# A fused retention, two-expert mixture and SoLU kernel: the second expert's weights, rows and list places, and the last weights, in another order

## The chip, the cores and the metric

The kernel runs on one core of one Trainium2 chip, in one launch. The metric is the device time of one execution in microseconds (us), the median over runs. The core has five instruction streams that run in parallel and meet at semaphores: PE (TensorE, matmuls), DVE (VectorE), ACT (ScalarE), POOL (GpSimd) and SP (SyncE). Each stream is worked off strictly in the order in which it was written. SP, ACT and POOL also issue DMAs. An instruction that waits holds up all that stand behind it on the same stream.

## The reference

Three layers follow one another on 1536 tokens of 512 numbers (2 sequences of 768, 8 heads of 64).

```python
# 1. retention: a state per head that decays by gamma and takes k v^T at each step
for t in range(S):
    state = gamma * state + einsum('bhd,bhe->bhde', k[:, :, t], v[:, :, t])
    y[:, :, t] = scale * einsum('bhd,bhde->bhe', q[:, :, t], state)
x = y.transpose(0, 2, 1, 3).reshape(B * S, H * D)
# 2. mixture of 8 experts, two for each token, chosen by noisy logits
noisy_logits = x @ w_gate + log1p(exp(x @ w_noise)) * noise
top2, top2_w = two largest, softmax of the two
for e in range(8):
    out[mask] += top2_w[mask, k, None] * (maximum(x[mask] @ w1[e], 0) @ w2[e])
# 3. SoLU block: 512 -> 1024 -> 512
h = x @ w_in
solu = h * softmax(h)
ln = (solu - mean) / sqrt(var + 1e-6) * g_ln
return ln @ w_out
```

`w_in` and `w_out` come as 64-bit floats and are converted on DVE while the experts run (`convert()`). Every weight and every operand of the two large layers is split into a high and a low part, and each product is three matmuls (high by high, high by low, low by high).

## The kernel before

**Units.** The weights are 72 units of 512 KB, eight for each expert (four of `w1`, four of `w2`) and eight for the last layer. `load_unit` starts the DMA of a raw unit (tile `wr`, four buffers), `split_unit` makes the high part `wh` on ACT (L202) and the low part `wl` on DVE (L203); ten split units fit. `feed(split_to, load_to)` advances both counters, and `advance(e, j)` calls it once for each quarter of an expert. A load can start only when the split of the unit four before it has released the buffer. Which expert runs when is known only from the counts: `turns()` orders the experts (`turn_ix`), and from expert 1 on the address of a load comes from a register that the issuing engine reads from `turn_ix` (L170). Units 8 to 11, the `w1` of expert 1, are issued by POOL; all others by SP.

**Attention**, 12 tiles of 128 tokens, one turn of the loop at L708 for each tile i: `from_state` (old state times queries), `kv` (state update, L435; copied by ACT as `S`), `from_chunk` (L449, with the masked scores `pm`; DVE scales its result to `xT`, L451, by a table `fade` that ACT makes in `table(c)`, L368), `scale_v(i + 2)` (the values times their decay, one half on POOL, the other on ACT), `scores(i + 1)` (L405, masked by DVE at L409), and `rows_logits(i)` (L461: turns the tile into rows and makes its logits; ACT copies both out, and SP stores the rows to `xd`). Between these stand the steps of the choice of experts, for four groups of tiles (0 to 3, 4 to 7, 8 and 9, 10 and 11): `route(g)`, called four times for each group (logits and noise; first half of a polynomial; its second half and the two largest, which gives `chosen`; their indices), `rank(g)` (PE counts places, L582), `slots(g)` (DVE works out the place of each token in its expert's list), `first_rows(g)` (DVE marks the tokens of expert 0, tiles `oh`, L527) and `scatter(i)` (POOL writes a tile's token numbers to the lists, two indirect DMAs).

**Expert 0** starts early: 192 of its rows come from tiles 0 to 7 (`list_rows(0)` finds them by matmuls with `oh`, POOL gathers them, `first_xt(0, .)` turns them on PE) and run through `w1` in one full-precision pass, `hidden(0, f, ...)` for f = 0 to 7 (L671 with `xe`). Its later 256 rows are listed and turned meanwhile (`list_rows(1)`, `first_xt(1, .)`, split on DVE at L572), and follow as eight more `hidden` steps with split operands. Each `hidden` step ends with `hh` on ACT (L675) and `hl` on DVE (L676); for expert 0 they use two buffers of bank `b`.

**Experts 1 to 7.** `second(e, j)`, j = 0 to 3, is an expert's second product (L1030, eight steps of 12 matmuls). During it the next expert's rows are made ready: `load_xg` on POOL (list entries, then rows; for expert 1 four gathers `xr`, L975), and `xg_t(e + 1, d)`, d = 0 to 3, which for expert 1 turns the rows on PE into bank `a` (two buffers), with ACT (`xh`, L995) and DVE (`xl`, L996) behind it. Only then does `hidden(e + 1, ...)` start.

**The end.** The last expert's results are made as rows (L1115, b = 0 to 2), stored to `yg` (L1101), gathered for each token by POOL (`gather`, L751), mixed (`mix`, ACT L761 and DVE L762), turned (`x2_t`, L771) and sent through the last layer, 12 tiles, in a software pipeline. The last two units of weights (four rows of `w_out` blocks) are split by `last_weights` into room that expert 7's operands leave.

Of the kernel before, what the change touches and what calls it, by code (L numbers as in the profile page):

```python
# [44 lines left out]
def retnet_moe_solu(ctx, tc, qT, kT, k, v, w_gate, w_noise, noise, w1, w2, w_in, w_out, g_ln,  # L45
# [110 lines left out]
    def load_unit(u):  # L156
# [7 lines left out]
        q = nc.gpsimd if e == 1 and j < 4 else nc.sync  # L164
        if e == E:
            wa, wb = w_in, w_out
        else:
            wa, wb = w1, w2
            if e and (e, q) not in turn_of:
                turn_of[e, q] = nc.values_load(turn_ix[:1, e:e + 1], engines=[q.engine], min_val=0, max_val=E - 1)  # L170
            n = bass.DynSlice(turn_of[e, q], 1) if e else slice(0, 1)
            wa, wb = (w[n].rearrange("o r c -> (o r) c") for w in (wa, wb))
# [105 lines left out]
    for half in range(2):  # L278
# [8 lines left out]
                   allow_small_or_imprecise_dtypes=True)  # L287
    number = const.tile([128, NT], F16, name="number")
# [107 lines left out]
    def scores(i, between=None):  # L396
# [9 lines left out]
        if between:  # L406
            between()
# [64 lines left out]
    def choose(g):  # L472
# [3 lines left out]
        t = rt.tile([128, 8, 4, E], F32, tag="rt", name="rt")  # L476
        th, r, ab, nl = (t[:, n, :m] for n in range(4))
        lg = rt.tile([128, 4, 2 * E], F32, tag="lg", name="lg")[:, :m]
# [15 lines left out]
        ix = rt.tile([128, 4, 8], U32, tag="ix", name="ix")  # L494
# [7 lines left out]
        pk = rt.tile([128, 4, 2, E], F32, tag="pk", name="pk")  # L502
# [9 lines left out]
    def first_rows(g):  # L512
# [10 lines left out]
        for s in range(m):  # L523
# [3 lines left out]
            V.tensor_scalar(t[:, lo:], col[:, lo:], s0[:, s:s + 1], None, op0=OP.is_equal)  # L527
# [173 lines left out]
    ROUTE = {3: (0, 0), 4: (0,), 5: (0,), 7: (1, 1), 8: (1,), 9: (2,), 10: (2,)}  # L701
    SCATTER = {5: (0,), 6: (1,), 7: (2,), 8: (3,)}
# [5 lines left out]
    for i in range(NT):  # L708
# [5 lines left out]
        from_chunk(i)  # L714
        if i == 11:
            route(2)
        scale_v(i + 2)
        scores(i + 1, (lambda: list_rows(0, range(EARLY_TILES), "a0")) if i == 10 else None)
        rows_logits(i)
        if i == 5:  # L720
            rank(0, "a1")
        if i == 9:
            rank(1, "a1")
            first_rows(1)
        if i == 11:
# [147 lines left out]
    def last_weights():  # L873
# [5 lines left out]
        for n in range(4):  # L879
# [30 lines left out]
    route(1)  # L910
    route(3)
    first_xt(0, 0)
    first_xt(0, 2)
    first_rows(2)
    slots(1)
    for n in range(4, 6):
        scatter(n)
    route(3)
    route(3)
    raw0 = [raw_t[d] for d in range(KD)]  # L920
    for f in range(KF):
        evacuate = hidden(0, f, slice(0, EARLY), ("c0", "c1", "b", "b")[f % 4])
        if f == 1:
            list_rows(1, range(NT - 2), "a1")
# [10 lines left out]
        if f == 4:  # L935
            route(2)
            slots(2)
            scatter(8)
            scatter(9)
        if f == 5:  # L940
            route(3)
            slots(3)
            scatter(10)
            scatter(11)
    feed(4, 8)
    for p in range(2):
        first_xt(1, 2 * p)
    turns()
# [72 lines left out]
    def second(e, j, py):  # L1021
# [20 lines left out]
    for e in range(E - 1):  # L1042
# [51 lines left out]
    feed(n_units - 2, n_units)  # L1094
# [9 lines left out]
    conv_ctx.close()  # L1104
    m2_ctx = ExitStack()
    fr = m2_ctx.enter_context(tc.tile_pool(name="fr", bufs=2, side="right", reuse_waits="tile"))
    for b in range(3):
# [26 lines left out]
    solu(0)  # L1134
    x2_t(2)
# [6 lines left out]
    z_turn(1)  # L1142
# [170 lines left out]
```

## Time and profile before

| | |
|---|---|
| median of 3 runs | 537.77 us (546.83, 537.77, 534.22) |
| the profiled execution | 533.07 us, its span 531.4 us |
| granted TensorE clock, mean over the span | 0.976 of full speed |
| PE busy | 505.0 us (95%) |
| DVE busy | 373.8 us (70%) |
| ACT busy | 217.6 us (41%) |
| POOL busy | 190.1 us (36%) |
| chain that ended last | PE 73%, DMA 3%, issue 2%, POOL 1%, DVE 1% |

The span is from the first to the last instruction; the execution's own time has 1.7 us more around it. "Busy" counts what an engine worked on; a matmul whose operands are late is not busy, one that runs at the lower clock is busy for twice as long. The clock is granted at one of two levels, 2.4 GHz (1.00) and 1.2 GHz (0.50); a value between them in a stretch means that both were granted in it. Stages by the timeline: attention to about 62 us, expert 0's early rows to 81, its later rows to 99, its second product and the turn of expert 1's rows to 130, experts 1 to 7 to 363, the rest the last expert's rows and the last layer.

### The profile page before, as it was taken

To read this page: it belongs to the slowest core of one execution; us is meant where nothing else is said; L and a number is where in the kernel's file an instruction comes from. 1 tells how busy PE (TensorE), PEld (TensorE's weight loads), DVE (VectorE), ACT (ScalarE), POOL (GpSimd) and SP (SyncE) were. 2 spreads that over 40 slices of the span, in tenths; PEclk is the share of its full clock that TensorE was granted. 3 is DMA by queue.
4 is the path that set the end of the run, shared out by engine and by line. 5 is a ranking of instruction groups with operands and counts; after the bars stand their busy time and mean duration, and the time that the engine had idled before them with its cause. 6 is when DMAs were issued, how large, how long until landed. Compare 5 with 4: busy or idle time off the path is not lost.

```text
span 531.4 us, 8949 instructions
## 1 busy us (share of the span) xinstructions
PE 505.0 (95%) x3216; PEld 459.3 (86%) x3216; DVE 373.8 (70%) x741; ACT 217.6 (41%) x426; POOL 190.1 (36%) x291
## 2 busy tenths in 40 slices
PE   8989897967999999999999999999799999999996
PEld 7877787957999999999999999998578888888885
DVE  4487867635888986987888879885348865666640
ACT  4565342432432442434434334435425543343441
POOL 3126258657475715507327000000423523311120
PEclk9999978997999999999999999999989999999999
DMA  8899407087576695766867857667522754553331
GB/s 249 303 303 345 156 22 257 21 270 255 199 179 218 229 269 187 221 177 222 237 224 227 245 178 203 197 164 222 174 85 81 223 172 141 162 175 100 99 120 45
DMA packets 60130, 100.36 MB, mean 189 GB/s; under 512 B 10896, under 2 KB 28400, under 8 KB 60080
## 3 DMA queue, kind: packets, MB, share of 16 engines
q1 hardware_dynamic: 52144, 83.84, 50.9%
q0 software_dynamic: 6592, 15.54, 9.9%
q8 instruction: 27, 0.44, 0.3%
q10 hardware_dynamic: 1344, 0.34, 0.3%
q14 instruction: 23, 0.19, 0.1%
HBM read 76.99 MB, written 22.70 MB: 188 GB/s over the span
## 4 chain that ended last, share of the span: by engine, by line
PE 73%; DMA 3%; issue 2%; POOL 1%; DVE 1%; ACT 0%; POOLq 0%; ACTq 0%; DVEq 0%
PE c L1030 22%; PE d L790 13%; PE b L897 12%; PE b L671 12%; PE a L671 12%; DMA wr<-in_moe_w_dram 1%; PE c L1115 1%; PE a L771 1%; DMA yg<-y 1%; DMA y<-yg,slot_y 1%; DVE wl L203 0%; POOL y L751 0%; PE a L843 0%; POOL wr L184 0%; PE a L989 0%
## 5 line engine op out<-in xcount | busy, mean ns | idle before, releaser
L975 POOL DMA_INDIRECT xq<-xd,rows x78 | 86.2, 1106 | 61.0 <-issue 60.3
L203 DVE TENSOR_TENSOR wl<-wr,wh 128x1024 fp32r<-128x1024 f32 x68 | 81.8, 1220 | 12.1 <-ACT wh L202 11.8
L1030 PE MATMUL c<-hh,wh 128*128 128x448 f32 (+5 forms) x224 | 79.8, 356 | 0.0
L1030 PE MATMUL c<-hl,wh 128*128 128x448 f32 (+5 forms) x224 | 79.5, 355 | 0.0
L1030 PE MATMUL c<-hh,wl 128*128 128x448 f32 (+5 forms) x224 | 79.4, 355 | 0.0
L202 ACT ACTIVATE wh<-wr 128x1024 fp32r<-128x1024 f32 x68 | 69.9, 1050 | 13.4 <-DMA wr<-in_moe_w_dram 12.1
L751 POOL DMA_INDIRECT y<-yg,slot_y x24 | 24.0, 1001 | 92.4 <-DMA yg<-y 86.7
L671 PE MATMUL b<-xh,wh 128*128 128x256 f32 (+7 forms) x144 | 48.0, 339 | 2.5 <-DVE hl L676 2.3
L671 PE MATMUL b<-xh,wl 128*128 128x256 f32 (+7 forms) x144 | 47.6, 337 | 0.0
L1030 PEld LDWEIGHTS c<-hh,wh 128*128 128x128 f32 x224 | 42.7, 191 | 1.2
L1030 PEld LDWEIGHTS c<-hh,wl 128*128 128x128 f32 x224 | 42.6, 190 | 1.2
L1030 PEld LDWEIGHTS c<-hl,wh 128*128 128x128 f32 x224 | 42.6, 190 | 1.2
L790 PE MATMUL d<-wh,x2h 128*128 128x512 f32 x96 | 40.1, 418 | 0.3 <-ACT x2h L774 0.3
L675 ACT ACTIVATE hh<-b 128x256 fp32r<-128x256 f32 (+8 forms) x40 | 18.7, 467 | 52.7 <-PE b L671 52.5
L790 PE MATMUL d<-wh,x2l 128*128 128x512 f32 x96 | 39.0, 406 | 0.2 <-DVE x2l L775 0.2
L671 PE MATMUL a<-xh,wh 128*128 128x448 f32 (+6 forms) x112 | 39.0, 348 | 0.0
L671 PE MATMUL a<-xh,wl 128*128 128x448 f32 (+6 forms) x112 | 38.9, 347 | 0.0
L790 PE MATMUL d<-wl,x2h 128*128 128x512 f32 x96 | 38.7, 404 | 0.0
L995 ACT ACTIVATE xh<-xt 128x428 fp32r<-128x428 f32 (+5 forms) x24 | 13.0, 540 | 56.1 <-DVE xt L993 56.1
L675 ACT ACTIVATE hh<-a 128x448 fp32r<-128x448 f32 (+6 forms) x28 | 14.3, 512 | 47.0 <-PE a L671 47.0
L817 POOL TENSOR_SCALAR st<-st 128x1 f32<-128x1 f32 x12 | 2.3, 190 | 85.4 <-ACT ee L814 85.4
L671 PE MATMUL b<-xl,wh 128*128 128x256 f32 (+7 forms) x144 | 31.2, 339 | 0.2 <-DVE xl L572 0.2
(226 smaller groups left out, 1114.9 us busy)
## 6 DMA issues: line engine op xcount, KB each, us to landing
wr<-in_moe_w_dram SPq DMA_DIRECT2D x60, 512.0 KB, 5.6
zd<-zs SPq DMA_DIRECT2D x40, 128.0 KB, 2.3
zc<-zd SPq DMA_DIRECT2D x10, 512.0 KB, 4.0
raw<-in_moe_w_in_dram SPq DMA_DIRECT2D x8, 512.0 KB, 5.0
raw<-in_moe_w_out_dram SPq DMA_DIRECT2D x8, 512.0 KB, 4.8
yg<-yr SPq DMA_DIRECT2D x16, 208.0 KB, 3.9
qt<-in_qT_dram SPq DMA_DIRECT2D x12, 256.0 KB, 4.7
vt<-in_v_dram SPq DMA_DIRECT2D x12, 256.0 KB, 5.4
```

Of the source, the lines that this page charges most:

```text
L202: nc.scalar.activation(hi, t, AF.Copy)
L203: nc.vector.tensor_sub(lo, t, hi)
L671: nc.tensor.matmul(p, w[:, 0, f * 128:(f + 1) * 128], x[:, d, c], start=(n == 0), stop=(n == len(terms) - 1))
L675: nc.scalar.activation(hh[:, f, c], p, AF.Relu)
L751: nc.gpsimd.indirect_dma_start(out=t, out_offset=None, in_=yg[:upto], in_offset=bass.IndirectOffsetOnAxis(ap=slot_y[:, i, s:s + 1], axis=0))
L771: nc.tensor.transpose(p[:, d * 128:(d + 1) * 128], t[:, d * 128:(d + 1) * 128], ident)
L790: nc.tensor.matmul(PH[i][:, s, :], x[:, c], w[:, 0, f], start=(n == 0), stop=(n == 3 * KD - 1))
L897: nc.tensor.matmul(p, z[:, f * 128:(f + 1) * 128], w_rows(f, n)[:, c], start=(m == 0), stop=(m == len(terms) - 1))
L975: nc.gpsimd.indirect_dma_start(out=x[:, b] if e > 1 else xr_t[e][b], out_offset=None, in_=src[:], in_offset=bass.IndirectOffsetOnAxis(ap=r ...
L995: nc.scalar.activation(hi, t, AF.Copy)
L1030: nc.tensor.matmul(py[d][:, :CAPS[e]], c, h[:, f, :CAPS[e]], start=(f == 0 and n == 0), stop=(f == KF - 1 and n == 2))
L1115: nc.tensor.matmul(py, h[:, f, c], w[:, f % 2], start=(f == 0 and n == 0), stop=(f == KF - 1 and n == 2))
```

## The change

The diff cut to its core. Line numbers after `@@` are those of the two files.

```diff
@@ load_unit
-        q = nc.gpsimd if e == 1 and j < 4 else nc.sync
+        q = nc.sync
...
@@ constants
+    col_h = const.tile([128, CAPS[0]], F16, name="col_h")
+    nc.vector.tensor_copy(col_h, col)
...
@@ first_rows
-            V.tensor_scalar(t[:, lo:], col[:, lo:], s0[:, s:s + 1], None, op0=OP.is_equal)
+            V.tensor_scalar(t[:, lo:], col_h[:, lo:], s0[:, s:s + 1], None, op0=OP.is_equal)
...
@@ the loop over attention's tiles
-    ROUTE = {3: (0, 0), 4: (0,), 5: (0,), 7: (1, 1), 8: (1,), 9: (2,), 10: (2,)}
-    SCATTER = {5: (0,), 6: (1,), 7: (2,), 8: (3,)}
+    SCATTER = {6: (0,), 7: (1,), 8: (2,), 9: (3,), 10: (4,), 11: (5,)}
...
         from_state(i)
         kv(i)
-        from_chunk(i)
-        if i == 11:
-            route(2)
-        scale_v(i + 2)
-        scores(i + 1, (lambda: list_rows(0, range(EARLY_TILES), "a0")) if i == 10 else None)
-        rows_logits(i)
-        if i == 5:
+        if i == 6:
             rank(0, "a1")
         if i == 9:
             rank(1, "a1")
+        if i == 11:
+            route(2)
+        from_chunk(i)
+        if i == 1:
+            table(1)
+        if i == 11:
+            rank(2, "a1")
+            first_xt(0, 0)
+            first_xt(0, 2)
+            first_rows(2)
+        scores(i + 1)
+        rows_logits(i)
+        if i and i % 2 == 0 and i + 2 < NT:
+            table(i // 2 + 1)
+        if i in (3, 4, 5, 6):
+            route(0)
+        if i == 6:
+            slots(0)
+        if i == 7:
+            route(1)
+            first_rows(0)
+        if i in (7, 8):
+            route(1)
+        if i == 9:
             first_rows(1)
-        if i == 11:
-            rank(2, "a0")
-        for g in ROUTE.get(i, ()):
-            route(g)
-        if i == 5:
-            slots(0)
-        if i == 6:
-            first_rows(0)
-        if i % 2 and i + 1 < NT:
-            table((i + 1) // 2)
+            route(2)
+            route(1)
+            list_rows(0, range(EARLY_TILES), "a0")
+        if i == 10:
+            slots(1)
+            route(2)
+        scale_v(i + 2)
         for n in SCATTER.get(i, ()):
             scatter(n)
-        feed(0, max(0, min(i - 4, 4)))
+        feed(0, max(0, min(2 * (i - 7), 4)))
...
@@ expert 0, after hidden_of(0)
-    route(1)
     route(3)
-    first_xt(0, 0)
-    first_xt(0, 2)
-    first_rows(2)
-    slots(1)
-    for n in range(4, 6):
-        scatter(n)
+    route(2)
     route(3)
     route(3)
+    scatter(6)
...
         if f == 3:
             list_rows(1, range(NT - 2, NT))
-            scatter(6)
-            scatter(7)
+            slots(2)
+            for n in range(7, 10):
+                scatter(n)
         evacuate()
         if f > 2:
             feed(min(f - 2, 4), 0)
-        if f == 4:
-            route(2)
-            slots(2)
-            scatter(8)
-            scatter(9)
-        if f == 5:
-            route(3)
-            slots(3)
-            scatter(10)
-            scatter(11)
     feed(4, 8)
     for p in range(2):
         first_xt(1, 2 * p)
+    route(3)
+    slots(3)
+    scatter(10)
+    scatter(11)
     turns()
...
@@ second(e, j, py, between=()), behind the first of its two steps
+            if s == 0:
+                for d in between:
+                    xg_t(e + 1, d)
...
-            second(e, j, py)
-            for d in (((0, 1), (2,), (3,), ()) if e else ((), (), (0, 1, 2), (3,)))[j]:
+            second(e, j, py, (0, 1) if j == 3 and not e else ())
+            for d in (((0, 1), (2,), (3,), ()) if e else ((), (), (), (2, 3)))[j]:
                 xg_t(e + 1, d)
...
@@ the end: the last two units are loaded at b == 1, behind the first two stores of y, ...
-    feed(n_units - 2, n_units)
+    feed(n_units - 2, n_units - 2)
...
         if b == 0:
             for i in range(FRONT_TILES):
                 gather(i, OFF[e] + 128)
-            last_weights()
         if b == 1:
+            feed(n_units - 2, n_units)
             mix(0)
             mix(1)
...
     solu(0)
+    last_weights((0, 1))
     x2_t(2)
...
     z_turn(1)
+    last_weights((2, 3))
     h_in(2, 0)
```

Besides, four small tiles of `choose` get a third buffer. Three places in the order of the instructions carry the prediction's terms. In the rows below L-numbers are lines of each file, `x4` stands for four alike in a row.

The first place is the handover to expert 1, on the queues that issue its weights. On POOL, before: list entries, gathered rows, then the register and the loads of `w1`.

```order
L655 DMA token_of<-token,slot 7168x1
L960 DMA rows<-token_of,at_r 128x4
L975 DMA xr<-xd,rows 128x512 x4
L170 TENSOR_LOAD turn_ix
L170 ISA x2
L184 ISA
L184 DMA wr<-in_moe_w_dram 128x1024
```

On SP, in the changed kernel, behind the loads of expert 0's `w2` (L184, 128x2x512) and two raw blocks of the conversion:

```order
L184 DMA wr<-in_moe_w_dram 128x2x512 x4
L108 DMA raw<-in_moe_w_in_dram 128x512 x2
L170 TENSOR_LOAD turn_ix
L170 ISA x2
L184 ISA
L184 DMA wr<-in_moe_w_dram 128x1024
```

The four loads of 128x1024 left POOL, where they stood behind the gathers of expert 1's rows, for SP, where they stand behind the raw blocks.

The second place is DVE at the end of expert 0's early rows: before, where `xl` (L572) is the split of its later rows and `keys` the start of `turns()`.

```order
L203 TENSOR_TENSOR wl<-wr,wh 128x1024
L500 MAX_INDEX ix<-top,rt 128x8 x2
L501 CAST top_i<-ix 128x4
L503 TENSOR_TENSOR pk<-e_161,top_i 128x32
L595 TENSOR_TENSOR pk<-pk,a_1229 128x32
L596 TENSOR_REDUCE ranks<-pk 128x4
```

The same group of steps in the changed kernel, for the last group of tiles:

```order
L572 TENSOR_TENSOR xl<-a_1470,xh 128x2x256
L572 TENSOR_TENSOR xl<-a_1477,xh 128x2x256
L500 MAX_INDEX ix<-top,rt 128x8 x2
L501 CAST top_i<-ix 128x4
L503 TENSOR_TENSOR pk<-e_161,top_i 128x32
L595 TENSOR_TENSOR pk<-pk,c_1362 128x32
L596 TENSOR_REDUCE ranks<-pk 128x4
L598 TENSOR_SCALAR sets<-ranks 128x4
```

The steps of the last two groups stood between the weight splits and ahead of `xl`; now those of tiles 8 and 9 stand ahead of the first weight split, and those of tiles 10 and 11 behind `xl` and ahead of `turns()`.

The third place is DVE at attention's last tile. Before:

```order
L409 TENSOR_TENSOR pm<-b,causal 128x512 x2
L485 SCALAR_TENSOR_TENSOR rt<-rt 128x16
L486 TENSOR_SCALAR rt<-rt 128x16
L490 SCALAR_TENSOR_TENSOR rt<-rt 128x16 x4
L451 TENSOR_TENSOR xT<-c_1186,fade 128x256
L451 TENSOR_TENSOR xT<-c_1187,fade 128x256
L490 SCALAR_TENSOR_TENSOR rt<-rt 128x16 x3
```

In the changed kernel:

```order
L603 SCALAR_TENSOR_TENSOR slot<-rt 128x8
L485 SCALAR_TENSOR_TENSOR rt<-rt 128x16
L486 TENSOR_SCALAR rt<-rt 128x16
L490 SCALAR_TENSOR_TENSOR rt<-rt 128x16 x7
L491 SCALAR_TENSOR_TENSOR rt<-rt 128x16
L492 TENSOR_TENSOR rt<-rt,nz 128x16
L493 TENSOR_TENSOR rt<-rt,lg 128x16
L496 MAX top<-rt 128x8 x2
L497 TENSOR_TENSOR chosen<-rt,top 128x16
L451 TENSOR_TENSOR xT<-c_1206,fade 128x256
L451 TENSOR_TENSOR xT<-c_1207,fade 128x256
```

The places of tiles 4 to 7 (`slots(1)`, which ends at `slot`) and the whole choice for tiles 8 and 9 now stand ahead of the last tile's `xT`.

## Rows read from the trace of the kernel before

**Rows 1.** Waits of PE: line, releaser, us in total, times, longest.
```profile
PE a L989 <- DVE xl L996: 7.5, 1, 7.5
PE c L461 <- DVE xT L451: 3.1, 4, 1.4
PE a L771 <- DVE t L762: 2.6, 1, 2.6
PE b L671 <- DVE hl L676: 2.3, 1, 2.3
```

**Rows 2.** Timeline of PE, expert 0's second product: start, us, instruction [idle before].
```profile
99.29 0.37 PE L1030 MATMUL c<-hh,wh 128*128 128x448 f32 x1
...
113.88 1.03 PE L989 MATMUL a<-ident,xr 128*128 128x128 f32 x8
...
130.18 0.45 PE L671 MATMUL b<-xh,wh 128*128 128x448 f32 x1
```

**Rows 3.** Timeline of POOL, the same stretch.
```profile
108.11 2.21 POOL L184 DMA_DIRECT2D wr<-in_moe_w_dram  x4
```

**Rows 4.** Timeline of ACT, the same stretch.
```profile
113.08 1.06 ACT L202 ACTIVATE wh<-wr 128x1024 fp32r<-128x1024 f32 x1 [11.31 <-DMA wr<-in_moe_w_dram]
```

**Rows 5.** Timeline of DVE, the same stretch: splits of units 4 and 7, then rows.
```profile
94.70 1.22 DVE L203 TENSOR_TENSOR wl<-wr,wh 128x1024 fp32r<-128x1024 f32 x1 [0.52 <-ACT wh L202]
...
103.59 1.21 DVE L203 TENSOR_TENSOR wl<-wr,wh 128x1024 fp32r<-128x1024 f32 x1
...
121.73 1.14 DVE L996 TENSOR_TENSOR xl<-a,xh 128x448 fp32r<-128x448 f32 x2
```

**Rows 6.** DMA issues: queue, count, KB each, median us to landing.
```profile
wr<-in_moe_w_dram SPq DMA_DIRECT2D x60, 512.0 KB, 5.6
```

**Rows 7.** Timeline of PE, attention and expert 0's hidden steps.
```profile
48.54 1.25 PE L461 MATMUL c<-unit,xT 128*128 128x144 f32 x8 [0.91 <-DVE xT L451]
...
50.83 1.05 PE L449 MATMUL c<-pm,vs 128*64 128x128 f32 x16
...
55.88 1.16 PE L405 MATMUL b<-qt,kt 64*128 64x128 f32 x16
...
67.94 4.21 PE L671 MATMUL c<-xe,wr 128*128 128x192 f32 x12 [0.94 <-ACT xe L565]
...
78.36 2.76 PE L671 MATMUL b<-xe,wr 128*128 128x192 f32 x16
...
90.25 0.28 PE L671 MATMUL b<-xh,wh 128*128 128x256 f32 x1
```

**Rows 8.** Timeline of DVE, attention.
```profile
48.74 1.28 DVE L409 TENSOR_TENSOR pm<-b,causal 128x512 f32<-128x512 f32 x2
49.93 0.64 DVE L490 SCALAR_TENSOR_TENSOR rt<-rt 128x32 f32<-128x32 f32 x3
...
51.69 0.19 DVE L497 TENSOR_TENSOR chosen<-rt,top 128x32 bf16<-128x32 f32 x1
...
54.56 1.90 DVE L527 TENSOR_SCALAR oh<-col,s 128x448 f16<-128x448 f32 x4
```

**Rows 9.** Windows: us, PE, PEld, DVE, ACT, POOL busy, granted clock, DMA share, GB/s.
```profile
30.00:40.00 10.00, 9.94 (x156) 8.71 (x156) 9.16 (x40) 5.67 (x24) 2.62 (x6) 1.00 0.91 292
...
66.00:68.00 2.00, 1.06 (x5) 0.56 (x3) 1.51 (x11) 0.70 (x3) 0.56 (x1) 0.50 0.00 0
```

**Rows 10.** Timeline of DVE, expert 0: places of tiles 8 and 9, then `xl`, `turns()`, `hl`.
```profile
79.71 0.08 DVE L500 MATCH_VALUE_LOAD ix<-top,rt 128x8 f32 x1
...
81.53 0.16 DVE L603 SCALAR_TENSOR_TENSOR slot<-rt 128x4 uint32<-128x4 f32 x1
...
86.57 1.28 DVE L572 TENSOR_TENSOR xl<-a,xh 128x512 fp32r<-128x512 f32 x2
...
89.30 0.42 DVE L676 SCALAR_TENSOR_TENSOR hl<-b,hh 128x256 fp32r<-128x256 f32 x1
```

**Rows 11.** Stores and gathers of the tile `y`: the stores' last line.
```profile
DMA to landing us min/median/max: 3.6/4.5/4.9
```

More of the change, by code (lines that the diff above doesn't have):

```diff
@@ L168, in load_unit @@
             wa, wb = w1, w2
-            if e and (e, q) not in turn_of:
-                turn_of[e, q] = nc.values_load(turn_ix[:1, e:e + 1], engines=[q.engine], min_val=0, max_val=E - 1)
-            n = bass.DynSlice(turn_of[e, q], 1) if e else slice(0, 1)
+            if e and e not in turn_of:
+                turn_of[e] = nc.values_load(turn_ix[:1, e:e + 1], engines=[q.engine], min_val=0, max_val=E - 1)
+            n = bass.DynSlice(turn_of[e], 1) if e else slice(0, 1)
             wa, wb = (w[n].rearrange("o r c -> (o r) c") for w in (wa, wb))
@@ L394, in scale_v, with scores @@
         VS[i] = t
-    def scores(i, between=None):
+    def scores(i):
         if i >= NT:
@@ L405, in scores @@
                 nc.tensor.matmul(p[s][:, hp, :], KT[i][r, hp, :], QT[i][r, hp, :], start=True, stop=True)
-        if between:
-            between()
         for s in range(2):
@@ L475, in choose @@
         ii = slice(i0, i0 + m)
-        t = rt.tile([128, 8, 4, E], F32, tag="rt", name="rt")
+        t = rt.tile([128, 8, 4, E], F32, tag="rt", name="rt", bufs=3)
         th, r, ab, nl = (t[:, n, :m] for n in range(4))
-        lg = rt.tile([128, 4, 2 * E], F32, tag="lg", name="lg")[:, :m]
+        lg = rt.tile([128, 4, 2 * E], F32, tag="lg", name="lg", bufs=3)[:, :m]
         V = nc.vector
@@ L493, in choose @@
         V.tensor_add(nl, nl, lg[:, :, :E])
-        ix = rt.tile([128, 4, 8], U32, tag="ix", name="ix")
+        ix = rt.tile([128, 4, 8], U32, tag="ix", name="ix", bufs=3)
         for n in range(m):
@@ L501, in choose @@
         V.tensor_copy(top_i[:, ii, :], ix[:, :m, :2])
-        pk = rt.tile([128, 4, 2, E], F32, tag="pk", name="pk")
+        pk = rt.tile([128, 4, 2, E], F32, tag="pk", name="pk", bufs=3)
         V.tensor_tensor(pk[:, :m], e8[:, None, None, :].to_broadcast([128, m, 2, E]),
@@ L723, in retnet_moe_solu @@
             rank(1, "a1")
-            first_rows(1)
-        if i == 11:
-            rank(2, "a0")
-        for g in ROUTE.get(i, ()):
-            route(g)
-        if i == 5:
-            slots(0)
-        if i == 6:
-            first_rows(0)
-        if i % 2 and i + 1 < NT:
-            table((i + 1) // 2)
+        if i == 11:
[22 more added lines that the diff above has]
+        if i == 9:
+            first_rows(1)
+            route(2)
[5 more added lines that the diff above has]
+        scale_v(i + 2)
         for n in SCATTER.get(i, ()):
             scatter(n)
-        feed(0, max(0, min(i - 4, 4)))
+        feed(0, max(0, min(2 * (i - 7), 4)))
+    att.close()
     att.close()
@@ L871, in retnet_moe_solu, with last_room @@
     late_rows = {}
-    def last_weights():
+    def last_room():
         room = [px.tile([128, KD, CAP], F32R, tag=t, name=t).rearrange("p d n -> p (d n)") for t in ("xh", "xl")]
@@ L878, in last_weights @@
             t.append(px.tile([128, DM], F32R, tag="xr", name="xr", bufs=4))
-        for n in range(4):
+        return room
+    def last_weights(ns):
+        for n in ns:
             f = KF - 4 + n
@@ L923, in retnet_moe_solu @@
         if f == 1:
-            list_rows(1, range(NT - 2), "a1")
+            list_rows(1, range(NT - 2), "a0")
         if f == 2:
@@ L1019, in y_t, with second @@
             PY.pop(e)
-    def second(e, j, py):
+    def second(e, j, py, between=()):
         hh, hl = H_t[e]
@@ L1104, in retnet_moe_solu @@
     conv_ctx.close()
+    room = last_room()
     m2_ctx = ExitStack()
```

## The prediction

> **What bounds the kernel now.** I read the busy shares first: PE 95%, no other engine over 70%, and the chain that ended last is PE for 73%. So the time is PE's, and a change can give back only PE's waits and its stretches at the lower clock. The list of PE's waits [rows 1] names where: 7.5 us once for `xl` of expert 1, 3.1 in four pieces for attention's `xT`, 2.6 for the first mixed tile, 2.3 for an `hl` of expert 0. From 130 us to 363 PE never waits; the change has nothing to win there and only has to keep it so.
>
> The largest wait I followed back through the timelines. PE turned half of expert 1's rows at 113.88 [rows 2] and then needed a buffer of bank `a`, which DVE's `xl` at 121.73 set free [rows 5]. DVE and ACT were late because the splits of `w1` stand ahead of these rows on both, and ACT had sat 11.3 us until the first of these units landed, at 113.08 [rows 4]. POOL had issued it at 108.11 [rows 3], after expert 1's gathers. But the buffer had been free since DVE ended the split of unit 4, at 94.70 + 1.22 = 95.9 [rows 5]. The head of the chain is an in-order queue, and this is the queue that the change takes the loads off.
>
> **1. The handover to expert 1: -9.4 us.** Call 99.29 T, the start of expert 0's second product [rows 2]. By 113.88 three quarters of its 96 matmuls had run, 14.59 us, so all take 19.45; eight transposes take 1.03, sixteen 2.06. PE's own work is 21.5 us, but `hidden` of expert 1 starts at 130.18, T + 30.9. The rest, 9.4, is the wait of 7.5 and 1.9 of half speed behind it. It goes if ACT and DVE have done their splits before PE turns the rows. On SP the load of unit 8 can go at T - 3.4 (unit 4's split ends) and that of unit 11 at T + 5.5 (unit 7's split ends, 103.59 + 1.21 [rows 5]). With 5.6 us to landing [rows 6] and 1.06 + 1.22 us for the split [rows 4, 5], unit 11 is split at T + 13.4. Units 12 and 13 are split ahead of the rows too. Unit 13 waits for the split of unit 9, whose load goes between these two, at about T - 0.5, so that it is split at T + 7.4; unit 13 lands at T + 13.0 and is split at T + 15.3. The turns now stand behind the seventh eighth of the product, T + 17.0, and a buffer is needed again after one more step (2.4) and the turns, at T + 20.5. Spare: 1.7 us for the splits, some 2 more for the buffer. The gathers hide as before: PE did not wait for them at 113.88. So I take all of it; the other end is -5 (rival 2).
>
> The Trainium skill ("Trainium Kernel Development and Optimization", Key Constraints) says that DMAs from SP, ACT and POOL run on the same 16 engines, and that issuing from several queues saves only issue time. That speaks against this edit; by it the sum would be the rival at 530.9 below. The row that bears on it: 12.2 us between free buffer and issue is not issue time but a queue that waits for other things.
>
> **2. Attention: +0.8 us.** `rank(0)` and `rank(1)` now stand ahead of `from_chunk`, one tile after the step that gives `chosen`. From the start of a tile's scores PE is there after 1.16 (scores) and 2.29 (logits, state, kv: 48.54 to 50.83), at 3.45 [rows 7]. DVE ends `pm` at 1.16 + 0.1 + 1.28 = 2.5, and the step takes 49.93 to 51.69 + 0.19, 1.95, so 4.5 [rows 8]. PE waits 1.05, twice: +2.1. `list_rows(0)` stands behind tile 9's logits (at 1.16 + 1.2 = 2.3), its marks `oh` behind `pm`: 2.5 + 0.2 + 1.90 = 4.6 with the four marks at today's price [rows 8]: +2.3. The marks read 16-bit numbers now; I keep today's price, since no row has this form, and nothing below zero follows from it.
>
> By the Trainium skill ("VectorE: DVE Perf Modes", What auto-detection actually checks) an all-16-bit operation of this kind runs at four elements a cycle; an estimate from that page's figures is 0.27 us a mark, and the sum would be 0.8 us lower.
>
> Against this, tables come two tiles ahead and the choice is spread over single tiles: two waits for `xT` ahead of tile 11's scores go, 1.4 + 0.9 [rows 1, 7]: -2.3. At the last tile, from its scores (before at 55.88): `pm` at 2.5, `slots(1)` about 1.3, both halves of the polynomial for two tiles about 2.8, so `chosen` at 6.6; `rank(2)` 0.4, eight transposes 0.9, logits 1.2: the early rows of expert 0 start at 9.1. PE waits 3 us in this. Before, 4 of their 64 matmuls had run at 67.94; at 2.76 for 16 [rows 7] that is a gapless start at 67.2, or 11.3, with the list's matmuls in it, about 0.9, now paid earlier. 9.1 + 0.9 - 11.3: -1.3. Sum +0.8; ends -1.5 (waits half as long) and +2.5 (lower clock once in attention).
>
> **3. From expert 0's early rows to its later ones: -1.5 us.** Before, 67.2 to the third later step at 90.25 [rows 7] is 23.05. After, four early steps at 1.4 with rank and list are over at 7; places of tiles 8 and 9 about 1.3; four splits 4 x 1.22 and five `hl` of 0.35 bring DVE to 14.9, `xl` (1.28) to 16.2. Places of tiles 10 and 11 with their indices (79.71 to 81.69, 2.0), `turns()` (87.85 to 89.30, 1.45) and `hl` (0.42) [rows 10] follow: 20.0. Two groups of 2.0 no longer stand ahead of `xl`, but one now stands between `xl` and the `hl` that frees bank `b`, for which the third later step waits. PE would be there at 18.0: **the wait of 2.3 [rows 1] is not removed but moved**, and is 2.0. I add 1.5, since the clock will be low for some of this as it was at 66 to 68 (0.50 [rows 9]): 21.5. Ends -3.0 (no lower clock) and 0.
>
> **4. The clock behind that new wait: +0.8.** Between 0 and the 1.9 that half speed cost behind the 7.5 us wait; nearer the lower end, as the wait is a quarter as long.
>
> **5. The end: -0.7 us.** The first store of `y` no longer follows 1 MB of weights on SP: 4.9 us can become 3.6 [rows 11], -1.3, in the 2.6 us that PE waits [rows 1]. The same 1 MB now goes beside the gathers that the wait ends on; I give half back. The four splits of `last_weights`, half of 1.22 each on DVE [rows 5], 2.4 us, move from idle time to the first tiles' softmax; DVE (70% busy over the span) covers them with its later idle time. Without that cover +2.4 is the upper end; the lower is -2.6 with 1.9 of half speed gone behind it.
>
> Scatters on POOL cost nothing: the last four still wait for places, and expert 1's gathers need them only by T + 17. The cast of `col` to 16 bits stands in DVE's idle start.
>
> **Sum.** -9.4 + 0.8 - 1.5 + 0.8 - 0.7 = -10.0, from the profiled execution's 533.07: 523.1. That execution is the fastest shown: the timed ones are 1.2 to 13.8 above it, their median 4.7. I add the smallest distance: **524 us**.
>
> **Rivals.** (1) *Everything closes* (2 in 20): parts 3 and 5 at their lower ends: 533.07 - 9.4 + 0.8 - 3.0 - 4.5 = 517. For it: all these waits are short and clocked down behind, so each pays twice; against it the new waits counted above.
>
> (2) *A wait takes the place of the one removed* (4 in 20). SP's loads and the gathers share 16 engines; if units 9 and 13 need twice the 5.6 us, unit 13 is split at T + 26.5 and `xl` frees bank `a` at T + 27.7 instead of T + 20.5. With half of that much delay, the likelier case, PE waits 3.5 us and loses 1 more to the clock: 528. For it: ACT and DVE have 1.7 us to spare; against: unit 11 has 7 us.
>
> (3) *The queue is not it*, the skill's rule (1 in 20): the loads would be bound by the DMA engines whichever queue issues them, and only POOL's 2.21 us of issue [rows 3] are saved: 530.9.
>
> (4) *Slower* (1 in 20): PE's new pauses in attention bring the clock down each time. Before, the pauses around 62 to 68 did: 12 matmuls took 4.21 instead of 2.07, and with the four before them some 3.1 us were lost [rows 7]. Four pauses (two `rank`, list, `rank(2)`) at 3.1, less the 1.5 already in part 3: 523.1 + 10.9 = 534, or 535 beside the timed runs. It decides from the third pause on. Against it: a pause of 1.4 us [rows 1], which ended at 30.1, left the clock at 1.00 [rows 9].
>
> **The numbers.** Forecast 12 in 20 (520 to 528), rivals as above. Range 517 to 531: it leaves out rival 4 and the far ends. 2% of the median, about what a measurement can tell from no change, is 527.0: below lie most of the forecast, rival 1, little of rival 2: faster 0.57, within 0.41, slower 0.02.
>
> **What would show it.** Right: no wait over 1 us at the turn of expert 1's rows, `wh` of unit 8 before 103 us by T = 99, `hidden` of expert 1 at T + 21.5; waits of about 1 us at both `rank`, 2 at the list, 3 at `rank(2)`, 2 for `hl` at the third later step. Wrong: splits of units 12 or 13 still running when PE has turned the rows; the clock at 0.50 between 36 and 60 us; PE idle on `x2l` or `zl` after 390.

## The result, and the profile after

The changed kernel took 539.12 us (median of 20, 535.85 to 549.10), beside 541.41 for the kernel before. The ratio, with its 95% interval, is 1.012 [1.009, 1.014]: **1.2% slower**, less than the 2% from which a change is counted, where 524 (517 to 531) and most likely a gain were forecast. Of the twenty times of the kernel before nine lie from 529 to 535 us, one at 537.77 and ten from 545 to 557, and only the nine enter the ratio. The profiled execution took 540.02 us, its span is 538.3 and its mean granted clock 0.974 (before: 533.07, 531.4, 0.976).

The waits of PE in it, to be read against [rows 1]:

```profile
PE b L671 <- DVE hl L676: 8.6, 1, 8.6
PE a L582 <- DVE top L496: 3.5, 1, 3.5
PE d L805 <- ACT x2h L789: 3.3, 1, 3.3
PE c L461 <- DVE xT L451: 2.4, 1, 2.4
PE a L582 <- DVE chosen L497: 2.2, 2, 1.3
PE b L561 <- issue: 1.8, 2, 1.0
```

The 7.5 us at the handover are gone, as forecast. But the wait for `hl` at the first later rows, forecast at 2.0, is 8.6. At the last attention tile 2.4 for `xT` and 1.8 of "issue", in which PE halts and waits for nothing that the profile shows, follow the 3.5 for the choice.

Who was late there? For the first place, the timelines of PE, DVE, ACT and POOL (start, us, instruction [idle before <- releaser]):

```profile
63.36 1.16 PE L449 MATMUL c<-pm,vs 128*64 128x128 f32 x16 [0.35 <-issue]
68.00 0.17 PE L582 MATMUL a<-chosen,before 128*128 128x16 bf16 x1 [3.47 <-DVE top L496]
...
68.46 0.48 PE L561 MATMUL b<-ident,xr 96*128 96x96 f32 x2
...
71.33 1.03 PE L561 MATMUL b<-ident,xr 96*128 96x96 f32 x4 [0.86 <-issue]
74.77 2.26 PE L461 MATMUL c<-unit,xT 128*128 128x144 f32 x8 [2.41 <-DVE xT L451]
```
```profile
67.77 0.18 DVE L497 TENSOR_TENSOR chosen<-rt,top 128x16 bf16<-128x16 f32 x1
74.20 0.76 DVE L451 TENSOR_TENSOR xT<-c,fade 128x256 f32<-128x256 f32 x2 [6.26 <-remote]
```
```profile
74.55 0.49 ACT L565 ACTIVATE xe<-b 128x384 f32<-128x384 f32 x1 [10.75 <-remote]
```
```profile
62.68 1.03 POOL L655 DMA_INDIRECT token_of<-token,slot  x1 [0.18 <-issue]
...
71.61 0.96 POOL L655 DMA_INDIRECT token_of<-token,slot  x1 [0.22 <-issue]
```

DVE's `xT` needs one thing only, PE's matmuls at 63.36, and these were over by 64.5. DVE was free from 67.95 on and sat until 74.20; ACT sat as well, until 74.55, for transposes that were over by 72.36. "Remote" says that the profile found no instruction that ended just before the release. The trace's own record of PE's signals (the semaphore updates at an instruction's end, on which others wait) shows why: the eight that were due from 63.80 to 72.36 are recorded from 72.76 to 74.53, the third at 74.18, and `xT` starts at 74.20. In the trace before, 269 of PE's 272 recorded signals come within 0.05 us of a matmul's end, and the other three stand behind PE's last matmul. From 62.68 on stand eight scatters of POOL, 0.3 us apart, the last of which ends at 72.57. The other direction was open: `chosen` ended on DVE at 67.95 and PE went on at 68.00.

The second place, under the first later steps, reads the same:

```profile
93.38 0.76 PE L671 MATMUL b<-xl,wh 128*128 128x256 f32 x4
...
104.12 0.58 PE L671 MATMUL b<-xh,wh 128*128 128x256 f32 x1 [8.55 <-DVE hl L676]
```
```profile
103.22 0.66 ACT L675 ACTIVATE hh<-b 128x256 fp32r<-128x256 f32 x2 [10.48 <-remote]
```
```profile
88.78 1.13 POOL L655 DMA_INDIRECT token_of<-token,slot  x1 [0.23 <-issue]
...
100.55 0.96 POOL L655 DMA_INDIRECT token_of<-token,slot  x1 [0.22 <-issue]
```

PE's first later step ended at 94.14; ACT learned it at 103.2, after ten scatters back to back. The `hl` for which PE waits is late because `hh` is, and `hh` because PE's own signal is. It is not memory traffic that the two places share: by the windows (columns as in [rows 9]) the DMA engines were busy for 0.02 of the first stretch, but for 0.97 of the second up to 100 us.

```profile
66.00:74.00 8.00, 2.48 (x18) 1.50 (x17) 1.60 (x10) 0.00 (x0) 5.47 (x11) 0.54 0.02 0
...
92.00:100.00 8.00, 3.56 (x37) 3.23 (x34) 4.55 (x26) 0.75 (x2) 6.69 (x13) 1.00 0.97 363
100.00:108.00 8.00, 3.88 (x19) 3.88 (x20) 1.18 (x3) 1.04 (x3) 3.35 (x6) 0.57 0.02 0
```

### The profile page after: what moved, and what is told of

It reads as the page before. It is cut to its first block, busy times and chain, and to the rows that moved or that the text cites. A ratio compares the mean times of both kernels' runs of the same rounds, so it can differ in the third digit from the quotient of the medians.

```text
span 538.3 us, 8946 instructions
## 1 busy us (share of the span) xinstructions
PE 504.6 (94%) x3216; PEld 459.6 (85%) x3216; DVE 372.5 (69%) x742; ACT 218.7 (41%) x426; POOL 190.8 (35%) x287
## 4 chain that ended last, share of the span: by engine, by line
PE 82%; DMA 6%; DVE 4%; another core or an unknown queue 3%; issue 2%; ACT 1%; POOL 0%; SPq 0%; POOLq 0%; ACTq 0%; DVEq 0%
PE c L1038 24%; PE b L671 14%; PE b L915 12%; PE a L671 12%; PE d L805 11%; PE c L461 2%; PE b L407 1%; DMA y<-yg,slot_y 1%; PE c L449 1%; PE c L1127 1%; DMA qt<-in_qT_dram 1%; PE a L786 1%; DMA xr<-xd,rows 1%; PE c L671 1%
## 5 line engine op out<-in xcount | busy, mean ns | idle before, releaser
L983 POOL DMA_INDIRECT xq<-xd,rows x78 | 91.2, 1169 | 65.9 <-issue 65.3
L676 DVE SCALAR_TENSOR_TENSOR hl<-b,hh 128x256 fp32r<-128x256 f32 (+8 forms) x40 | 20.9, 524 | 22.4 <-ACT hh L675 16.6
L671 PEld LDWEIGHTS b<-xh,wh 128*128 128x128 f32 x144 | 28.0, 194 | 9.5 <-DVE hl L676 9.1
```

Of the source, the lines that this page charges most:

```text
L671: nc.tensor.matmul(p, w[:, 0, f * 128:(f + 1) * 128], x[:, d, c], start=(n == 0), stop=(n == len(terms) - 1))
L676: nc.vector.scalar_tensor_tensor(hl[:, f, c], p, 0.0, hh[:, f, c], op0=OP.max, op1=OP.subtract)
L983: nc.gpsimd.indirect_dma_start(out=x[:, b] if e > 1 else xr_t[e][b], out_offset=None, in_=src[:], in_offset=bass.IndirectOffsetOnAxis(ap=r ...
```

## The experiments

Three theories stood at first: **A**, POOL's queue without any direct transfer brings the late signals about; **B**, the new order in attention does; **C**, they follow no edit but the chip or the execution. The fifteen runs were made on five chips, e1 to e4 on one, then e5 and e6, e7 to e9, e10 to e12, e13 to e15. Each is compared with runs of the kernel before on the same chip.

**e1**, the kernel before with the queue alone:

```
-        q = nc.gpsimd if e == 1 and j < 4 else nc.sync
+        q = nc.sync
```

> The kernel before with one line changed: the four first weight pieces of the second expert on SyncE's queue. The trace of the changed kernel shows that TensorE's completion signals, which in the trace before arrive 0.02 us after the matmul's end, arrive up to 9 us late wherever GpSimd issues indirect transfers back to back (the matmul that ended at 94.14 is seen by ScalarE at 103.2). Theory A: GpSimd's queue without any direct transfer is what brings that about. Then this kernel has late signals too, and the handover's gain of about 7 us is eaten: 530 to 540 us. Theory B: the new order in attention brings it about (bursts of scatters placed where TensorE waits). Then no signal is later than 1 us here and the time is 533 - 7 to 533 - 9 = 524 to 526 us. Theory C: it is a condition of the single execution and follows no edit: it may appear here or not, and the time is 524 to 526 without it, some 8 to 12 us more with it.

Measured 526.02, ratio 0.989 [0.985, 0.992]; no late signals.

**e2**, the changed kernel with that line put back.

> The changed kernel with that one line undone: the four weight pieces of the second expert stand on GpSimd's queue again, all else as changed. Theory A (GpSimd's queue without direct transfers): the signals are on time again, the waits of 6.3 us at the last attention tile and 8.6 us in the later rows go, the handover's 7.5 us come back: 540 - 6 - 8.6 + 7.5 = about 533 us. Theory B (order in attention): the late signals stay and the handover's wait is added: 540 to 548 us. Theory C (condition of an execution): either, without regard to the edit.

Measured 526.85, 0.989 [0.983, 0.995]; no late signals.

**e3**, the changed kernel unaltered.

> The changed kernel once more, unaltered. Theories A and B: late signals at the same two places (over 5 us at the scatters of tiles 3 to 6 and of 7 to 11), 538 to 542 us. Theory C: if this execution has no late signals, the two waits are below 3 us and the time is 540 - 6 - 6 = about 526 to 530 us.

Measured 523.29, **0.983** [0.978, 0.989]; no late signals. A and B fall as sufficient causes: the kernel that had them in the recorded execution has none on this chip. Whether an edit has a part in them where they do appear, e1, e2 and e4 can't tell, since none of the three ran on a chip with late signals.

**e4**, attention and the early rows in the order of before, the rest as changed.

> The changed kernel with the attention's places and the early rows' order of the kernel before (the routing, the scatters and the second list stand where they stood), but with the weights on SyncE's queue, the 16-bit column numbers, the early rows turned inside the last step, and the last weights later. Theory A (GpSimd's queue without direct transfers): late signals, 532 to 540 us. Theory B (order in attention): signals on time, the handover's gain and that of the end are kept: 533.1 - 9.4 - 0.7 = about 523 us. Theory C: 523 without the condition, some 8 to 12 us more with it.

Measured 525.40, 0.987 [0.982, 0.993]; no late signals.

**e5 and e6**, both kernels unaltered on a second chip.

> The kernel before, unaltered, for its trace. If late completion signals are a condition of an execution or of a chip and follow no edit, they can stand in this trace as well: then the time is 545 to 557 us, as in the upper group of this kernel's twenty runs beside the changed kernel, and signals of TensorE come over 2 us late under its scatters (79 to 97 us). Without the condition: 529 to 537 us and at most one or two signals over 0.5 us late. If instead only the changed kernel's order can bring it about, this trace never shows it, whatever the time.

> The changed kernel, unaltered, once more, beside the kernel before. Condition of a chip or an execution: either both kernels show late signals here, with 545 to 557 us before and 536 to 542 us changed, or neither, with 529 to 537 and 521 to 525. Its two waits (the last attention tile's xT on VectorE, the first later step's hh on ScalarE) are over 5 us with it and below 1 us without.

Measured 532.48, 0.998 [0.995, 1.001], and 523.34, 0.982 [0.978, 0.986]; neither has late signals. In e6 PE waits for the choice and for `hl` as the prediction counted, and not at all at the handover; the waits for `x2h` and `xT` were not in the forecast:

```profile
PE a L582 <- DVE chosen L497: 4.9, 3, 2.7
PE d L805 <- ACT x2h L789: 2.7, 1, 2.7
PE b L671 <- DVE hl L676: 1.8, 1, 1.8
PE c L461 <- DVE xT L451: 1.4, 1, 1.4
```

Where the recorded execution's 16.6 us went is seen by starts of PE's work (us of each span), without late signals and with:

| | before, [rows 2, 7] | before, e5 | changed, e3 | changed, recorded |
|---|---|---|---|---|
| scores of tile 11 | 55.88 | 56.02 | 58.88 | 60.07 |
| early rows of expert 0, first matmul | 65.35 | 65.17 | 67.72 | 76.83 |
| third later step | 90.25 | 90.96 | 88.18 | 104.12 |
| second product, T | 99.29 | 100.85 | 97.31 | 114.79 |
| `hidden` of expert 1 | 130.18 | 130.00 | 118.43 | 135.91 |
| its second product | 149.72 | 149.92 | 137.97 | 155.45 |
| last matmul's end | 526.58 | 524.92 | 515.63 | 532.55 |

Between e3 and the recorded execution 1.2 us are lost ahead of tile 11, 7.9 at it, 6.8 at the early rows and the first later steps, and 1.5 up to T, at a low clock (0.57 granted from 100 to 108 us); from T to the end they agree within 0.6.

**e7 to e9** were meant for the end, where e3 waits 2.8 us for `x2h`. They met a chip on which all three traces have late signals. e7 is the changed kernel with its end as before; e8 moves one load, and e9 is e8 with three moves in attention:

```
         if b == 1:
-            feed(n_units - 2, n_units)
             mix(0)
             mix(1)
+        if b == 2:
+            feed(n_units - 2, n_units)
```
```
-        if i == 6:
-            rank(0, "a1")
-        if i == 9:
-            rank(1, "a1")
         if i == 11:
             route(2)
         from_chunk(i)
...
-            rank(2, "a1")
             first_xt(0, 0)
             first_xt(0, 2)
+            rank(2, "a1")
             first_rows(2)
         scores(i + 1)
+        if i == 6:
+            rank(0, "a1")
+        if i == 9:
+            rank(1, "a1")
```

> The changed kernel with its end as before: the last megabyte of weights is loaded ahead of the last expert's rows and split behind the first block of rows. In the undisturbed traces of the changed kernel TensorE waits 2.8 us for x2h and 1.1 for x2l at the first mixed tile: the gathers of the second mixed tile run beside that megabyte, ScalarE's t of that tile starts 5.7 us after its gather's issue and stands ahead of x2h. Theory: the moved weights cost about 3 us net (from the start of the third expert's product on, TensorE loses 5.3 us and gains 2.1 against the kernel before): 523.3 - 3 = 520 us here, x2h waited for under 1 us. Rival, the term of the prediction: the move saves 0.7 us, so 524 here.

> The changed kernel with the load of the last megabyte moved from behind the second to behind the third store of the last expert's rows. Theory (the load beside the gathers is what makes x2h late): the gather of the second mixed tile lands some 2 us after its issue, the waits of 2.8 and 1.1 us at x2h and x2l go to below 0.5 each, 523.3 - 3.5 = about 520 us, or 519 with the lower clock behind these waits gone too. Rival (the order on ScalarE alone makes x2h late, whatever loads): the waits stay over 2 us and the time is 523 us. A third way: the weights then come too late for the first split in the softmax of tile 1 and give 1 to 3 us back there: 521 to 523.

> As e8, and in attention the ranks of the first two groups stand behind the next tile's scores again, the transposes of the early rows ahead of the third rank. It takes away waits of 1.25 and 0.93 us and 0.86 of 2.70 us. Theory: a wait of TensorE in attention counts in full only if nothing later waits for VectorE or a gather at a fixed time; VectorE's chain of choices and places ends at the rows of the later tiles, where TensorE then waits longer for xr and hl. Then 1 to 1.5 us of the 3.0 remain: about 518.5 us. Rival: all of it counts, 516.5; or none, 519.5.

Measured 537.63, 1.005 [1.000, 1.009]; 538.39 (532.36 to 542.96), without a ratio; 529.95, 0.990 [0.976, 1.003]. No total came out as expected, since late signals stood in all three, and e7 takes 9.6 us more than e3 from expert 1's second product to the last matmul of the last expert's rows. e8's end can be compared by the stretch from the start of expert 1's second product to the last matmul's end, since the three traces agree up to the last expert's rows there (229.7 us each): 377.7 us in e3, 377.1 in the recorded execution, 372.2 in e8. In e3 (ACT, then PE):

```profile
369.27 0.72 ACT L776 ACTIVATE t<-y,top_w 128x512 f32<-128x512 f32 x1 [5.40 <-DMA y<-yg,slot_y]
369.89 0.58 ACT L789 ACTIVATE x2h<-a 128x512 fp32r<-128x512 f32 x1
```
```profile
366.39 0.60 PE L786 MATMUL a<-ident,t 128*128 128x128 f32 x4
...
370.52 0.50 PE L805 MATMUL d<-wh,x2h 128*128 128x512 f32 x1 [2.84 <-ACT x2h L789]
...
372.45 0.80 PE L805 MATMUL d<-wh,x2l 128*128 128x512 f32 x1 [1.12 <-DVE x2l L790]
```

and in e8:

```profile
382.71 0.60 PE L786 MATMUL a<-ident,t 128*128 128x128 f32 x4
...
385.01 0.50 PE L805 MATMUL d<-wh,x2h 128*128 128x512 f32 x1 [1.00 <-ACT x2h L789]
```

The second tile's `t` stands ahead of the first one's `x2h` on ACT, and its gather ran beside the megabyte that now follows the second store. With the load behind the third store the wait for `x2h` falls from 2.84 to 1.00 and that for `x2l` from 1.12 to 0.17, not below 0.5 each as expected. Most of the rest of the 5 us is the clock: behind these waits it was granted at 0.63 from 370 to 374 us and at 0.52 to 378 in e3, and at 1.00 from 380 to 395 in e8. All traces together bear the move out. From the last expert's last `hidden` step to the last matmul they take 162.7 to 164.8 us in the eight with the end of the changed kernel, 160.3 to 163.7 in the five with the end of before (e7 is one of them, at 163.7) and 158.2 to 159.7 in the four with the load moved (e8, e9, e13, e14).

**e10 to e12** take up the late signals where they are. e10 puts gaps into the first run of scatters; e11 and e12 are the two kernels unaltered:

```
             nc.gpsimd.memset(spacer, 0.0)
+            for _ in range(2 if 3 <= i <= 5 else 0):
+                nc.gpsimd.tensor_tensor(gap, gap, gap, op=OP.pow)
             st = nc.gpsimd.indirect_dma_start(
```

> The changed kernel with two tiny GpSimd operations (0.56 us each) ahead of each of the six scatters of tiles 3 to 5, so that some 1.4 us instead of 0.3 lie between them. The second burst (tiles 7 to 11, under the first later steps) is left as it is and serves as the control within the same run. Theory (on some chips TensorE's completion signals wait until a run of indirect transfers leaves a gap): on such a chip the wait for xT and xe at the last attention tile falls from 6 us to below 2, while the hh wait of about 9 us at the first later steps stays, and the time falls from about 539 to about 533. On a chip without late signals nothing is won, and up to 4 us are lost where the scatters now hold up the gather of the later rows: 523 to 527. Rival (the late signals depend on something else, such as memory traffic): both waits stay as they are.

> The changed kernel, unaltered, as the partner of the run with gaps on the same chip. On a chip with late signals 536 to 542 us with waits of about 6 and 9 us at the two places; without, 521 to 525 us.

> The kernel before, unaltered, for its trace on the same chip. If the late signals belong to the chip, its trace shows them exactly where the other two show them, TensorE's signals over 2 us late under the scatters between 67 and 97 us and under the gathers of the experts' rows, and the time is 533 to 558 us; on a chip without them 529 to 536 us.

Measured 534.99, 0.997 [0.991, 1.002], and 538.23, 1.009 [1.004, 1.015]. e11 has both waits again (`xT` 6.3 us, `hh` 9.1, "remote"). In e10 the first is gone (DVE, ACT, POOL):

```profile
67.47 0.75 DVE L451 TENSOR_TENSOR xT<-c,fade 128x256 f32<-128x256 f32 x2
```
```profile
69.44 0.49 ACT L565 ACTIVATE xe<-b 128x384 f32<-128x384 f32 x1 [6.33 <-PE b L561]
```
```profile
90.06 0.96 POOL L659 DMA_INDIRECT token_of<-token,slot  x1 [0.22 <-issue]
...
93.64 0.96 POOL L659 DMA_INDIRECT token_of<-token,slot  x1 [2.54 <-DVE best L614]
```

`xT` starts as soon as DVE is free, and `xe` 0.04 us after its transposes. The control failed: the second wait went as well. But its run of scatters had got a pause of 2.5 us by itself, and in this pause, at 93.19, ACT's `hh` started. That is the theory's own reading, yet no test of it. The total falls by 3 us only; a new wait of 3.9 us for a gather (`xr`), which stands behind the stretched run, takes part of the gain.

e12, the kernel before, has late signals too, in the one execution traced (555.74 us). It loses most of its time under the gathers of later experts' rows (ACT's waits):

```profile
ACT hh L675 <- remote: 38.5, 7, 9.6
```

From `hidden` of expert 1 to its second product PE needs 37.7 us there, 19.9 in e5. Its other executions on that chip took 530 to 540 and 545 to 555 us, and no trace shows what late signals do in the shorter ones. But the spread goes with them: over all its runs the kernel before took 529 to 537 us on the two chips without late signals and 530 to 559 on the three with them.

The same trace speaks against a simple rule. Its twelve scatters of tiles 6 to 11, from 79.69 to 96.36, stand under the first later steps as well and no further apart (ACT, then POOL):

```profile
89.03 0.38 ACT L675 ACTIVATE hh<-b 128x256 fp32r<-128x256 f32 x1 [5.50 <-PE b L671]
91.59 0.38 ACT L675 ACTIVATE hh<-b 128x256 fp32r<-128x256 f32 x1 [2.18 <-issue]
94.96 0.38 ACT L675 ACTIVATE hh<-b 128x256 fp32r<-128x256 f32 x1 [2.99 <-PE b L671]
```
```profile
89.08 0.96 POOL L655 DMA_INDIRECT token_of<-token,slot  x1 [0.23 <-issue]
...
90.35 0.96 POOL L655 DMA_INDIRECT token_of<-token,slot  x1 [0.22 <-issue]
...
91.61 0.96 POOL L655 DMA_INDIRECT token_of<-token,slot  x1 [0.23 <-issue]
```

PE's first two later steps ended at 88.99 and 91.55, and `hh` followed within 0.05 us in the middle of the run; the third and fourth `hh` came 1.9 and 3.4 us late, not 9. A dense run of transfers does not hold back every signal.

**e13** has e9's edits and one operation of 0.56 us ahead of each scatter of tiles 3, 4, 5, 8 and 9; **e14** is e9, **e15** the changed kernel, all on a third chip with late signals.

> As e9 (load of the last weights behind the third store, ranks behind the scores), with one tiny GpSimd operation (0.56 us) ahead of each scatter of tiles 3, 4, 5, 8 and 9, so that some 0.9 us lie between these instead of 0.3. Theory (TensorE's signals wait for a gap in GpSimd's indirect transfers, and the moved weights cost about 5 us beside the gathers of the mixed tiles): on a chip with late signals the waits at the last attention tile and at the first later step fall below 2 us each and the time is 519 to 525, against 530 for e9 and 538 for the changed kernel there; on a chip without them it is within 2 us of e9. Rival 1 (a gap of 0.9 us is too short): waits and time as in e9. Rival 2 (the second wait has another cause than the first): only the first falls, 524 to 530.

> The kernel of e9, unaltered, as partner on the same chip. With late signals 529 to 531 us as before. Without them: the three edits of e8 and e9 together take 523.3 - 5 (the end) - 1 to 3 (the ranks) to 515 to 517 us; if the ranks' waits are made up for by a longer wait for the rows of the later tiles, 518; if the end's gain showed only beside late signals, 521 to 523.

> The changed kernel, unaltered, as partner on the same chip: 536 to 543 us with late signals, 521 to 525 without.

Measured 522.60, **0.975** [0.965, 0.984]; 529.35, 0.987 [0.981, 0.994]; 538.54, 1.003 [0.999, 1.007]. e13 and e14 differ by the operations in the gaps alone, so these are worth some 7 us here (529.35 to 522.60), and the other edits the rest of the 16. PE's longest waits in e13, and POOL in its second run of scatters:

```profile
PE b L675 <- DVE hl L680: 1.9, 1, 1.9
PE b L561 <- DMA xr<-xd,rows: 1.4, 2, 1.2
PE c L461 <- DVE rt L490: 1.4, 1, 1.4
```
```profile
84.04 1.02 POOL L659 DMA_INDIRECT token_of<-token,slot  x1 [0.19 <-issue]
...
85.13 0.57 POOL L658 TENSOR_TENSOR gap<-gap 1x1 f32<-1x1 f32 x1
85.89 1.03 POOL L659 DMA_INDIRECT token_of<-token,slot  x1 [0.20 <-issue]
```

With 0.8 us between transfers ACT's `hh` starts at 84.13, 0.05 us after PE's step in the middle of the run, and both waits are below 2 us. So the gaps remove the second wait as they do the first, and 0.8 us is enough where 0.3 was not. e13 is the fastest kernel on a chip with late signals and beats both others there; on one without them it was not run.

## Why the prediction was wrong

**The step that failed** is one sentence behind the sum: "Scatters on POOL cost nothing: the last four still wait for places, and expert 1's gathers need them only by T + 17." I costed them as transfers with a due time. In the recorded execution and on three of the five chips they also hold back PE's signals (gaps between them end it, e13), and the change had put the run of tiles 3 to 6 under the last attention tile and that of tiles 7 to 11 under the first later steps, two places where PE soon needs the answer to a signal of its own. The first run is new there; at the second place the kernel before has a run too, which cost it less in e12. Part 2's 9.1 us from tile 11's scores to the early rows became 16.8, part 3's wait of 2.0 became 8.6, and 540.0 instead of 523.4 is these two, the clock behind them, and 1.2 us ahead of them.

No row of before showed late signals, but the times did show that something was not in the trace: three executions spread from 534 to 547 us, and I only added the smallest distance to the sum.

**Where signals are on time, the time came out** (e3 and e6: 523.3 us, forecast 524), **but in part by luck**. To the last matmul e3 gained 11.0 us on the profiled kernel before (526.58 to 515.63), where 10.0 were forecast; by its parts it is 9.8, -0.5, 2.6, -0.1 and -0.8, where 9.4, -0.8, 1.5, -0.8 and 0.7 were forecast. Parts 1 and 2 are near; the misses of 3 and 4 and that of 5 offset each other.

- Part 1: T to `hidden` of expert 1 takes 21.1 us in both (forecast 21.5; 30.9 [rows 2] and 29.2 in e5), and PE does not wait. The queue alone (e1) gives 1.1% [0.8, 1.5] of the forecast 1.8, but all other edits without it (e2) give as much: in e2 the handover's wait is down to 3.0 us as well, so the two overlap. The Trainium skill ("Trainium Kernel Development and Optimization", Key Constraints) has several queues save issue time alone; by that, the queue would give the 2.21 us of issue [rows 3]. e1, with 526.0 beside 532.3 for the kernel before, doesn't agree for a queue that is blocked by other work.
- Part 2: waits of 1.25 and 0.93 at the two ranks (1.05 each), 2.7 at the third (3), 8.8 us from tile 11's scores to the early rows (9.1). Two terms are mis-sized, and nearly cancel, which is luck. The two waits for `xT` were to go, 2.3 in all: the one of 1.4 did, but that of 0.91 at 48.54 [rows 7] became 1.42, so 0.9 came. And the list was to cost 2.3 and costs 0.3: eight of its sixteen matmuls start ahead of the four marks and need only older ones, and the four take 1.08 us instead of 1.90 [rows 8]. That is 0.27 each, which is the estimate from the Trainium skill ("VectorE: DVE Perf Modes", What auto-detection actually checks) that I had left out of the sum. In e3 (PE, then DVE):

```profile
48.70 1.22 PE L461 MATMUL c<-unit,xT 128*128 128x144 f32 x8 [1.42 <-DVE xT L451]
...
55.54 0.48 PE L539 MATMUL a<-number,oh 128*96 128x1 f16 x8
56.34 0.99 PE L539 MATMUL a<-number,oh 128*96 128x1 f16 x8 [0.32 <-DVE oh L527]
```
```profile
55.95 1.08 DVE L527 TENSOR_SCALAR oh<-col_h,s 128x448 f16<-128x448 f16 x4
```

- Part 3: 20.5 and 20.1 us from the early rows to the third later step (21.5), with a wait of 2.0 and 1.8 for `hl` (2.0). The clock did fall (0.67 granted from 68 to 72 us in e3), but the third later step waits for DVE all the same, so most of the 1.5 added for the clock did not count.
- Part 4: from the third later step to T both take 9.1 us, before 9.0 [rows 2, 7]; the 0.8 for a low clock behind the wait did not come (1.00 granted from 88 to 97 us in e3).
- Part 5 most likely has the wrong sign: -0.7 forecast. From expert 1's second product to the end the kernel before takes 376.9 and 375.0, the changed one 377.7 twice: a loss of 0.8 to 2.7. The other traces on these chips widen that: 373.7 with the end of before (e1), 376.0 and 376.5 with the changed one (e2, e4). I halved the gain for the megabyte beside the gathers; it makes the second tile's gather late, and ACT takes that tile ahead of `x2h`. Moved once more, it gives some 5 us (e8).

Rivals: (4), a lower clock through pauses, comes nearest with 534 but names a wrong cause: PE's short pauses at the ranks left the clock at 1.00 in e3, and in the recorded execution it fell at the two long waits. (1) needed gains in part 5, which lost; (2) and (3) fall with part 1.

**Open:** what makes the signals late, and whether it belongs to the chip or to the occasion, since each chip was used on one occasion only; why e12's run of scatters holds them back less than that of the changed kernel; why the kernel before pays for it in some executions only; and what e13 gains where signals are on time. One rival is untested: every time here comes with a span and a granted clock, so none was taken without the profiler, and the traces with late signals lack records all along from 40 to 440 us. Whether the recording has a part in the delay no run shows.

## What to carry to other kernels

Before a wait is explained by the engine it names, look at when that engine was free and when its producer ended: "remote" with both long over means that the signal itself was late. Where signals come late, keep long runs of GpSimd's indirect transfers away from places where TensorE hands results over through few buffers, or leave gaps between them (0.8 us was enough here). A spread of times that the profiled execution doesn't explain belongs into the range, and a surprising verdict is worth one more run of the same kernel on another chip before its edits are taken apart.

## What the runs showed of the hardware

- In the recorded execution and on three of five chips PE's signals were late under runs of POOL's indirect transfers 0.2 to 0.3 us apart, 9 us at the longest (due 94.14, recorded 103.20, after the run). With gaps of 0.8 us the waiting engines went on at once (e13); on the other two chips, the same program had its signals on time under the same runs. Not every such run holds every signal: in e12 two came on time in the middle of one. DVE's `chosen` released PE within 0.05 us in the middle of one.
- PE itself halts for some 0.9 us at a time while its signals are held ("issue", 1.8 us in two pieces in the recorded execution).
- The traces with late signals hold fewer update records: 6168 in the recorded execution, 8339 and 8355 for the same program in e3 and e6. They are missing all along, not at the scatters alone: from 40 to 140 us 820 are recorded beside 1812 in e3, from 140 to 240 us 852 beside 1703.
